# A third expert's products between the steps of a gated linear attention, with single buffers in exchange

## The chip, the cores and the metric

The kernel runs on one core of a Trainium2 chip. A core has five engines with a queue of instructions each: TensorE (PE: matrix products and, listed apart as PEld, the loads of their weights), VectorE (DVE), ScalarE (ACT), GpSimd (POOL) and SyncE (SP, which here issues nearly all DMAs). They wait for one another through semaphores. [...] The metric is the device time of one execution in microseconds (us).

## What is computed

A linear attention with a decaying state (4 batches, 8 heads, 768 tokens, head size 48), whose output is the input of eight dense experts (3072 tokens, width 384, inner width 1024), weighted by gates that a Sinkhorn iteration normalizes.

```python
for t in range(S):
    state = alpha[:, :, t, :, None] * state + einsum('bhd,bhe->bhde', k[:, :, t], v[:, :, t])
    y[:, :, t] = einsum('bhd,bhde->bhe', q[:, :, t], state)
...
logits = x @ w_gate                      # x: y with heads side by side
P = exp(logits - logits.max())
for _ in range(8):
    P /= P.sum(1, keepdims=True) + 1e-09
    P /= P.sum(0, keepdims=True) + 1e-09
    P *= N / E
for e in range(8):
    out += P[:, e:e+1] * (maximum(x @ w1[e], 0) @ w2[e])
```

## The kernel before

**Attention.** A unit is 256 tokens of a batch (12 units), a chunk 128 tokens (24 chunks, two a unit). For each unit `attn_block` (lines 238 to 377) loads q, k and alpha as `qt`, `kt`, `al` with a block of 16 tokens of one head on each partition, works out the scores inside the blocks over four levels (products on POOL or DVE as `tmp`, sums on DVE into `AB`, then `merge`), and puts the decayed q and k, the block decays (`ds`) and the scores through DRAM into another layout (`KN`, `QN`, `DN`, `an`); that put is its last step. It has 16 steps, each ended by a `yield`. `attn_decays` makes tables of decays from `DN` (the transpose psd on PE). `attn_chunk` (lines 419 to 534) has five steps for 128 tokens: transposes psk and psq and the decayed copies `decq`, `deck`; the products psl of whole blocks; the output psy, its largest value and the scaled copy `ys`; the transpose psx into `xT`, and the new state; the gate's logits psg (`lg`).

**Experts.** Values are split in two float16 halves, so each product is three. `moe_tile` (line 173) does one expert for a tile of tokens: eight groups of nine products `ps<-w,xT`, each taken out by ACT and DVE as the two halves `h`, and then, for each 128 tokens, 24 products of 384 columns `ps<-w,h`. Experts 0 and 1 are done while the attention runs, 256 tokens at a time, and their results go unweighted to DRAM (`raw`), since the gates aren't known yet. Their weights pass through the part of `xT` that late tokens will fill (lines 121 to 126). After the attention and the Sinkhorn iteration, experts 2 to 7 go in tiles of 512 tokens, one after the other; the first of them reads the two `raw` results of its tokens and weights them too (`evac_first`, line 679).

**Order.** While `hold` is set, every engine keeps program order. For the first chunks that order is written out by hand (START, line 39: `b1` a step of unit 1's block, `w0` one of expert 0's weights, `c0` one of chunk 0, `f` 0.45 us of the experts' products; a capital moves work from DVE to POOL). From chunk 3 on the loop of lines 608 to 626 takes five steps for each chunk, those of the chunk and the first two of the next in turn; after each step come two half steps, each with `fill(FILL / 2)`, which issues experts' products until their time by its count (0.96 us a piece) is used up, and `ahead`, which issues the steps of a later unit's block at fixed distances: its 16 steps begin 27 half steps ahead of its unit's first and end 12 ahead. `push` queues a unit's two tiles of 15.36 us, by the same count, at the third step of the unit's second chunk.

Of the kernel before, what the change touches and what calls it, by code (L numbers as in the profile page):

```python
# [8 lines left out]
F16 = mybir.dt.float16  # L9
# [10 lines left out]
EPS = 1e-9  # L20
# [3 lines left out]
def tile_gla_moe(ctx: ExitStack, tc: tile.TileContext, q, k, v, alpha, wg, w1, w2, out):  # L24
# [5 lines left out]
    U = 256                 # tokens of a unit of attention  # L30
    NU = S // U             # units of a batch
    NCH = U // P            # chunks of a unit
    KT_ = DM // P           # k tiles of the first product
    FT = FF // P            # f tiles
    NTT = NT // P           # token tiles
    NP = H // 2             # pairs of heads
    DP = 64                 # head dim, padded
    OFF = 28
    START = 'b1 W0 f W0 f f f w0 f f f f f f f c0 f f w0 W0 f B1 W0 b1 c0 f w0 f f W0 f c1 f f f f W1 f b1 c0 W0 c0 b1 f w0 w0 f f f w0 w0 f f c1 g b1 f f W1 c1 B1 W1 f f c0 f f b1 f f f f f f c1 f b1 f f B1 B1 f B1 W1 f f f f B1 B2 b1 w1 c1 f f f f f B1 w1 f b1 W1 W1 f f f w1 w1 w1 f b2 c2 w0 f w1 f f f B2 f f f f f B1 w1 W1 f f f w1 f f b2 f c2 B1 f f f f f f b2 f f w1 b2 f B2 f f f f B1 f b2 c3 f f f c2 b2 f f B2 f f B2 c3 f f f b2 f f c2 f B2 f B2 f f c2 f'.split()
    FILL = 3.0             # us of the experts' products between steps of the attention  # L40
# [5 lines left out]
    class Held:  # L46
        """an engine whose instructions stay in program order while hold is set"""
# [23 lines left out]
    cp = ctx.enter_context(tc.tile_pool(name="cp", bufs=1))  # L71
    sm = ctx.enter_context(tc.tile_pool(name="sm", bufs=4))
    wp = ctx.enter_context(tc.tile_pool(name="wp", bufs=2))

# [4 lines left out]
    mask = cp.tile([P, 8], F32, name="mask")          # mask[p, b] = (p // 16 == b)  # L79
# [10 lines left out]
    lg = cp.tile([P, NTT, E], F32, name="lg")          # logits, then P  # L90
    p2t = cp.tile([P, NTT], F32, name="p2t")           # power of two of each token
    wsc = cp.tile([P, E], F32, name="wsc")             # what undoes the scales of an expert

    def pow2_scale(mx, target, nm):
        """mx [P,1] >= 0 -> (float power of two <= mx, target / it)"""
# [15 lines left out]
    XT, W1T, W2T, WGT = 8.0, 4.0, 8.0, 8.0   # lower ends of the scaled maxima  # L111

    def load_expert(e, pool, res):
        """both weights of an expert, scaled and split into res; yields after its loads and each piece of work"""
        todo, pws = [], []
        for nm, w, target, C, W in (("w1", w1, W1T, KT_, FF), ("w2", w2, W2T, FT, DM)):
            src = w[e].rearrange("(c p) f -> p c f", p=P)
            hl = [wp.tile([P, C, W], F16, tag=f"{nm}{i}", name=f"{nm}{i}_{e}") for i in range(2)]
            n = -(-C // KT_)
            cut = [slice(i * n, min(C, (i + 1) * n)) for i in range(KT_)]  # L120
            if pool is None:
                # the first experts' weights pass through the room of late tokens
# [50 lines left out]
    def moe_tile(e, ws, t0, T, hp, evac):  # L173
        """yields the time of each piece of its products, in us"""
# [33 lines left out]
    raw = [dr.tile([NT, DM], F32, tag=f"raw{e}", bufs=1, name=f"raw{e}") for e in range(2)]  # L208
# [7 lines left out]
    hp1 = ctx.enter_context(tc.tile_pool(name="hp1", bufs=2))  # L216
# [6 lines left out]
    DN = [ap1.tile([16, H, DP], F32, name=f"DN{i}") for i in range(2)]  # L223
# [6 lines left out]

    for x in DN + ST:
        GE.memset(x, 0.0)
# [3 lines left out]
    ids = iter(range(1 << 20))  # L236

    def attn_block(b, u, got):
        """scores inside blocks of 16 tokens; a partition is a (block, head)"""
# [5 lines left out]
        qt = ap2.tile([P, 16, D], F32, tag="qt", name=f"qt_{nm}")  # L245
        kt = ap2.tile([P, 16, D], F32, tag="kt", name=f"kt_{nm}")
        al = ap2.tile([P, 16, D], F32, tag="al", name=f"al_{nm}")
# [6 lines left out]
        fast = g == 0                           # the first unit goes the shortest way  # L254
# [15 lines left out]
        def level(L):  # L270
            """what a level multiplies, and what then makes blocks of 2L"""
# [3 lines left out]
            # the decay over a block of L is kept at the block's first token  # L275
# [31 lines left out]
        if fast:  # L307
# [21 lines left out]
            for x in QN + KN:  # L329
                pool.memset(x[:, :, :, D:], 0.0)  # L330
        else:
            # what GpSimd multiplies is summed a step later
            t = mult(pool, "tmp4", [16], Af[:, 0:256:17], qt, kt)
            yield
            total(*t)
# [397 lines left out]
```

## Time and profile before

| | us |
|---|---|
| median of 3 runs | 1893.0 (1891.2 to 1894.6) |
| span of the profiled execution | 1885.1 |
| PE busy in it | 1722.3 |
| DVE busy | 893.8 |
| ACT busy | 464.4 |
| POOL busy | 346.3 |

The profile gives the profiled execution's span, from its first to its last instruction, and no total time of its own; the median of the runs lies 7.9 us above that span. Matmuls overlap in PE's pipeline, so a product's length in the trace is longer than its share of the time: how fast products follow one another is read from the starts in a timeline. Engines overlap too, so busy times don't add up to the span. [...]

### The profile page before, as it was taken

Reading aid. Unit: us, or ns where it says so; the run is one execution under the profiler, and the core shown is the slowest. Engines: PE = TensorE matmul, PEld = TensorE weight load, DVE = VectorE, ACT = ScalarE, POOL = GpSimd, SP = SyncE. Lnnn points to the kernel's source line nnn. Section 1 sums busy time; section 2 is a strip of 40 time slices with the busy share of each in tenths; the row PEclk is TensorE's granted clock in tenths of the full one; section 3 lists DMA queues with packets and bytes.
Section 4 is the critical chain, followed back from the end, with each engine's and each line's share of the span. In section 5 each row is a group of like instructions: output and inputs, shape, how many; then the busy total and the mean of one; then the engine's idle time right before and its main releaser. Section 6 shows DMA issues by size and latency. Waiting matters only on the chain.

```text
span 1885.1 us, 30215 instructions
## 1 busy us (share of the span) xinstructions
PE 1722.3 (91%) x13016; PEld 1064.5 (56%) x13016; DVE 893.8 (47%) x1723; ACT 464.4 (25%) x1008; POOL 346.3 (18%) x315
## 2 busy tenths in 40 slices
PE   0556889989889899999999999999999999999999
PEld 0435767767667786455555555555555555555555
DVE  6466766666676646952352235223423332323222
ACT  2232333333323242531221112111211121211111
POOL 4435545545455520000000000000000000000000
PEclk9867899999999999999999999999999999999999
DMA  6131233333333212640010001000100000000000
GB/s 177 57 82 46 50 89 91 87 88 92 91 76 79 68 37 85 210 134 0 34 34 1 1 34 34 1 1 34 34 1 1 1 1 1 1 1 17 34 17 34
DMA packets 143125, 92.20 MB, mean 49 GB/s; under 512 B 107152, under 2 KB 132240, under 8 KB 142992
## 3 DMA queue, kind: packets, MB, share of 16 engines
q1 hardware_dynamic: 142992, 90.28, 17.4%
q8 instruction: 102, 1.67, 0.4%
q14 instruction: 31, 0.25, 0.0%
HBM read 64.79 MB, written 25.46 MB: 48 GB/s over the span
## 4 chain that ended last, share of the span: by engine, by line
PE 65%; DVE 15%; DMA 7%; issue 5%; POOL 5%; ACT 2%; SPq 1%; POOLq 0%; ACTq 0%; DVEq 0%
PE ps L65 62%; POOL tmp L56 4%; DVE AB L56 3%; DMA kt<-in_k_dram 2%; DVE tmp L56 2%; DVE qt L56 2%; DMA ri<-raw 1%; DVE h L56 1%; PE psy L65 1%; DMA qs<-qt 1%; DVE decq L56 1%; DMA DN<-ds 1%; DVE w L56 1%; SPq L56 1%; DMA w2f<-in_moe_w_dram 1%
## 5 line engine op out<-in xcount | busy, mean ns | idle before, releaser
L65 PE MATMUL ps<-xT,w 128*128 128x512 f16 (+2 forms) x4392 | 785.1, 338 | 17.0 <-DVE h L56 11.1
L65 PE MATMUL ps<-w,h 128*128 128x384 f16 x4608 | 773.6, 328 | 10.6 <-DVE h L56 10.5
L65 PEld LDWEIGHTS <-w 128*128 128x128 f16 x4392 | 429.5, 100 | 351.0 <-issue 20.2
L65 PEld LDWEIGHTS <-h 128*128 128x128 f16 x4608 | 451.7, 98 | 308.5 <-issue 10.6
L56 ACT ACTIVATE h<-ps 128x512 f16<-128x512 f32 (+2 forms) x488 | 243.3, 505 | 898.8 <-PE ps L65 898.4
L56 DVE SCALAR_TENSOR_TENSOR h<-ps,h 128x512 f16<-128x512 f32 (+2 forms) x488 | 273.9, 574 | 362.8 <-ACT h L56 362.5
L56 DVE SCALAR_TENSOR_TENSOR acc<-ps,pe,acc 128x384 f32<-128x384 f32 x144 | 88.7, 616 | 360.7 <-PE ps L65 360.7
L56 POOL TENSOR_TENSOR tmp<-qt,kt 128x768 f32<-128x768 f32 (+1 forms) x88 | 152.2, 1734 | 152.7 <-DVE AB L56 61.7
L56 DVE TENSOR_REDUCE AB<-tmp 128x16 f32<-128x768 f32 (+2 forms) x105 | 94.6, 902 | 84.0 <-POOL tmp L56 83.5
L56 POOL PARTITION_ALL_REDUCE w1g<-w1m x8 | 2.9, 357 | 533.4 <-DVE w1m L56 521.8
L56 ACT COPY A<-psl 16x128 f32<-16x128 f32 (+2 forms) x168 | 56.0, 333 | 77.8 <-PE psl L65 66.4
L65 PE MATMUL psl<-decq,deck 48*32 48x32 f32 (+1 forms) x1152 | 33.7, 218 | 43.8 <-POOL deck L56 22.0
L65 PE MATMUL psy<-vn,A 128*128 128x48 f32 x384 | 58.1, 283 | 1.8 <-POOL w L56 1.8
L65 PEld LDWEIGHTS psy<-vn,A 128*128 128x128 f32 x384 | 54.9, 209 | 2.3 <-POOL w L56 2.2
L65 PEld LDWEIGHTS psl<-decq,deck 48*32 48x32 f32 (+1 forms) x1152 | 28.6, 129 | 46.3 <-POOL deck L56 22.6
L68 PE MATMUL psk<-ident,KN 128*128 128x128 f32 x96 | 17.4, 309 | 39.0 <-POOL KN L56 30.2
L56 POOL TENSOR_TENSOR kt<-kt,al 128x384 f32<-128x384 f32 x47 | 48.5, 1031 | 11.2 <-issue 7.1
L56 POOL TENSOR_TENSOR A<-an,mask 128x1024 f32<-128x1024 f32 x24 | 47.9, 1996 | 0.0
L56 DVE TENSOR_TENSOR qt<-qt,al 128x384 f32<-128x384 f32 (+1 forms) x55 | 46.4, 844 | 0.0
L56 ACT ACTIVATE ys<-psy,s_t 128x384 f32<-128x384 f32 x24 | 14.0, 581 | 131.4 <-DVE s_t L56 113.2
L65 PE MATMUL psy<-ST,Tq 128*128 128x96 f32 x160 | 35.2, 304 | 6.6 <-DVE wgm L56 6.2
L56 ACT COPY r<-ps 128x384 f32<-128x384 f32 x48 | 23.0, 479 | 69.3 <-PE ps L65 60.1
(139 smaller groups left out, 914.6 us busy)
## 6 DMA issues: line engine op xcount, KB each, us to landing
raw<-r SPq DMA_DIRECT2D x48, 192.0 KB, 1.9
w1f<-in_moe_w_dram SPq DMA_DIRECT2D x6, 1536.0 KB, 6.7
w2f<-in_moe_w_dram SPq DMA_DIRECT2D x6, 1536.0 KB, 6.9
ri<-raw SPq DMA_DIRECT2D x48, 192.0 KB, 2.5
qt<-in_q_dram SPq DMA_DIRECT2D x12, 384.0 KB, 4.3
al<-in_alpha_dram SPq DMA_DIRECT2D x12, 384.0 KB, 5.3
kt<-in_k_dram SPq DMA_DIRECT2D x12, 384.0 KB, 6.2
KN<-ks SPq DMA_DIRECT2D x24, 192.0 KB, 3.1
```

The costliest lines, as they stand in the source:

```text
L56: r = f(*a, **k_)
L65: tc.keep_in_program_order(nc.tensor.matmul(out_, lhsT, rhs, start=start, stop=stop))
L68: tc.keep_in_program_order(nc.tensor.transpose(out=out_, in_=in_, identity=idn))
```

## The change

NA = 3 experts are done beside the attention. The third one's weights come after START through the same part of `xT`, one step of `load_expert` after each step of a chunk from chunk 3 on, into a pool of their own (`wpa`). Its tiles wait in `late` until its weights are ready, and are queued with the others from then on, three tiles a unit. FILL goes from 3.0 to 4.7 us. To make room, `qt`, `kt`, `al`, `h`, `DN`, the decayed copies and `ys` have one buffer in place of two (the first unit's q, k and alpha are in a pool `first` that is closed early). A step of unit 2's block that START has ahead of unit 1's put now does that put. Sinkhorn has the load of expert 3 in front, and expert 3's preparation stands beside the last tiles. Five experts remain, and the first of them reads three `raw` results. The diff also drops comments; those lines are left out here.

```diff
-    FILL = 3.0             # us of the experts' products between steps of the attention
+    FILL = 4.7
+    NA = 3
...
+    early = ExitStack()
+    wpa = early.enter_context(tc.tile_pool(name="wpa", bufs=1, side="right"))
...
-            hl = [wp.tile([P, C, W], F16, tag=f"{nm}{i}", name=f"{nm}{i}_{e}") for i in range(2)]
+            hl = [(wpa if e == NA - 1 else wp).tile([P, C, W], F16, tag=f"{nm}{i}", name=f"{nm}{i}_{e}")
+                  for i in range(2)]
...
-    raw = [dr.tile([NT, DM], F32, tag=f"raw{e}", bufs=1, name=f"raw{e}") for e in range(2)]
+    raw = [dr.tile([NT, DM], F32, tag=f"raw{e}", bufs=1, name=f"raw{e}") for e in range(NA)]
...
-    hp1 = ctx.enter_context(tc.tile_pool(name="hp1", bufs=2))
...
-    DN = [ap1.tile([16, H, DP], F32, name=f"DN{i}") for i in range(2)]
+    DN = [ap1.tile([16, H, DP], F32, name="DN")] * 2
...
+    fst = ExitStack()
+    first = fst.enter_context(tc.tile_pool(name="first", bufs=1, side="right"))
...
-        qt = ap2.tile([P, 16, D], F32, tag="qt", name=f"qt_{nm}")
-        kt = ap2.tile([P, 16, D], F32, tag="kt", name=f"kt_{nm}")
-        al = ap2.tile([P, 16, D], F32, tag="al", name=f"al_{nm}")
+        qt, kt, al = ((first if g == 0 else ap1).tile([P, 16, D], F32, tag=x, name=f"{x}_{nm}")
+                      for x in ("qt", "kt", "al"))
...
-            t = ap2.tile([P, NP, m_ * L], F32, tag=f"dec{s}{L}", name=f"dec{s}{L}_{nm}")
+            t = ap2.tile([P, NP, m_ * L], F32, tag=f"dec{s}{L}", bufs=1, name=f"dec{s}{L}_{nm}")
...
-        ys = ap2.tile([P, DM], F32, tag="ys", name=f"ys_{nm}")
+        ys = ap2.tile([P, DM], F32, tag="ys", bufs=1, name=f"ys_{nm}")
...
-    wAB = [[], []]
-    w0, w1_ = (load_expert(e, None, wAB[e]) for e in range(2))
+    wAB = [[] for _ in range(NA)]
+    w0, w1_, w2_ = (load_expert(e, None, wAB[e]) for e in range(NA))
...
+    fst.close()
+    hp1 = early.enter_context(tc.tile_pool(name="hp1", bufs=1, side="right"))
...
-            advance(blocks[int(a[1])], 1)
-            done[int(a[1])] += 1
+            m = int(a[1])
+            if m == 2 and not got[1]:
+                m = 1
+            advance(blocks[m], 1)
+            done[m] += 1
...
+    late = [(2, 0, U)]
...
                 push((0, g * U, U), (1, g * U, U))
+                late.append((2, g * U, U))
             for z in range(2):
                 fill(FILL / 2)
                 ahead(10 * i + 2 * n + z)
+                if z and next(w2_, True):
+                    push(*late)
+                    late = []
...
-    w2_ = load_expert(2, wst, ws)
+    w3_ = load_expert(NA, wst, ws)
+    advance(w3_, 2)
     for n, _ in enumerate(sinkhorn()):
-        advance(w2_, n < 5)
         fill(2.8 if n else 4.0)
-    while len(filler) > 1:
+    while len(filler) > 3:
         fill(0.1)
     while filler:
-        advance(w2_, 1)
+        advance(w3_, 1)
         fill(1.0)
...
+    early.close()
+    hp2 = ctx.enter_context(tc.tile_pool(name="hp2", bufs=2, side="right"))
...
-        for i in range(2):
+        for i in range(NA):
...
-    for e in range(2, E):
+    for e in range(NA, E):
```

How instructions move is shown at three places. The first is POOL in the start, from the `p2t` or the last product of a level of unit 2's block to its later ones (`tmp_0_2_n` is the n-th product of that unit, `kt_2` its merge, `Tk_3` and `ST` belong to chunk 3). Before:

```order
L56 COPY p2t<-p_t_2_1284 128x1
L56 TENSOR_TENSOR kt_2_844<-kt_2_844,al_2_845 128x2x192
L56 TENSOR_TENSOR tmp_0_2_22_1322<-qt_2_843,kt_2_844 128x768
L56 TENSOR_TENSOR Tk_3_1235<-Tk_3_1235,k_0_1_988 128x512
L56 TENSOR_TENSOR ST_117<-ST_116,dtot_1_986 48x4x48 x2
L56 TENSOR_TENSOR tmp_0_2_23_1425<-qt_2_843,kt_2_844 128x768
```

And now:

```order
L57 TENSOR_TENSOR tmp_0_2_20_1304<-qt_2_975,kt_2_976 128x768
L57 TENSOR_TENSOR kt_2_976<-kt_2_976,al_2_977 128x2x192
L57 TENSOR_TENSOR tmp_0_2_21_1316<-qt_2_975,kt_2_976 128x1536
L57 TENSOR_TENSOR Tk_3_1238<-Tk_3_1238,k_0_1_992 128x512
L57 TENSOR_TENSOR tmp_0_2_22_1401<-qt_2_975,kt_2_976 128x768
L57 TENSOR_TENSOR ST_117<-ST_116,dtot_1_990 48x4x48 x2
L57 TENSOR_TENSOR tmp_0_2_23_1431<-qt_2_975,kt_2_976 128x768
```

The product of 1536 elements, `tmp_0_2_21`, stood on DVE before and is now POOL's, ahead of chunk 3's `Tk` and of the state `ST`.

The second is POOL in chunk 4, between two products of unit 3's block (`tmp_1_0_28` and `tmp_1_0_29`; `w1g` is a largest weight over all partitions, ISA alone a row without a name). Before:

```order
L56 TENSOR_TENSOR tmp_1_0_28_1782<-qt_0_1554,kt_0_1555 128x768
L56 COPY p2t<-p_t_4_1801 128x1
L56 TENSOR_TENSOR tmp_1_0_29_1824<-qt_0_1554,kt_0_1555 128x768
L56 TENSOR_TENSOR kt_0_1555<-kt_0_1555,al_0_1556 128x2x192
L56 TENSOR_TENSOR deck_0_5_1868<-Tk_5_1853,suf_124 128x256
```

And now:

```order
L57 TENSOR_TENSOR tmp_1_0_28_1835<-qt_0_1565,kt_0_1566 128x768
L57 ISA
L57 ISA w1g_1840<-w1m_2_1838 128x1
L57 COPY p2t<-p_t_4_1859 128x1
L57 ISA
L57 TENSOR_TENSOR tmp_1_0_29_1911<-qt_0_1565,kt_0_1566 128x768
L57 TENSOR_TENSOR kt_0_1566<-kt_0_1566,al_0_1567 128x2x192
```

The reduction of expert 2's first weights stands between them with a nameless row on either side; one for its second weights stands likewise ahead of chunk 6's `deck`.

The third is PE between the end of chunk 5's output (psy_5) and its transpose psx; `ps_e_t_m` are an expert's products for the tile from token t on, and psd, psk, psq belong to chunk 6. Before:

```order
L65 LDWEIGHTS h_1_256_1912
L65 MATMUL ps_1_256_1_2165<-w_1_622,h_1_256_1912 128x384
L68 MATMUL psd_0_2172<-ident,DN_115 128x16 x4
L68 MATMUL psk_0_2199<-ident,KN_113 128x128 x4
L68 MATMUL psq_0_2206<-ident,QN_111 128x128 x4
L65 LDWEIGHTS h_1_256_1911
```

And now:

```order
L66 MATMUL psy_5_2208<-ST_117,Tq_5_1965 128x96
L66 MATMUL psy_5_2208<-vn_2_1494,A_5_1975 128x48 x2
L69 MATMUL psd_0_2239<-ident,DN 128x16 x4
L69 MATMUL psk_0_2266<-ident,KN_114 128x128 x4
L69 MATMUL psq_0_2273<-ident,QN_112 128x128 x4
L69 MATMUL psx_5_2306<-ident,ys_5_2232 128x128 x3
```

Before, 18 products of expert 1 for the tokens from 256 on stand between psy_5 and psd, of which the last is shown, and more follow psq; now psd, psk, psq and psx follow psy_5 with none between. The same holds from the psl of chunk 5 on, but for 12 products right behind it.

## Rows read from the trace of the kernel before

**Rows 1.** The page's lines of the span and of PE, and the table of stretches: from and to (us), length, busy us of PE, PEld, DVE, ACT and POOL with their instructions, the granted clock of TensorE as a share of full speed, the mean busy share of the DMA engines, GB/s. The last row is one chunk near the end of the attention, from a call of its own.

```profile
span 1885.1 us, 30215 instructions
...
PE 1722.3 (91%) x13016; PEld 1064.5 (56%) x13016; DVE 893.8 (47%) x1723; ACT 464.4 (25%) x1008; POOL 346.3 (18%) x315
...
0.00:172.10 172.10, 78.42 (x936) 62.81 (x937) 109.07 (x187) 50.56 (x114) 84.30 (x88) 0.84 0.33 89
172.10:260.00 87.90, 71.32 (x818) 57.38 (x819) 50.47 (x99) 26.52 (x79) 35.75 (x32) 0.85 0.39 89
260.00:655.60 395.60, 353.43 (x4261) 278.37 (x4260) 271.79 (x507) 134.95 (x385) 211.87 (x172) 0.97 0.32 79
655.60:754.80 99.20, 96.74 (x958) 74.60 (x957) 53.94 (x159) 31.69 (x83) 10.54 (x14) 1.00 0.23 67
754.80:1881.30 1126.50, 1122.42 (x6050) 591.34 (x6047) 407.94 (x773) 220.73 (x348) 3.85 (x11) 1.00 0.08 27
...
667.46:689.31 21.85, 21.85 (x284) 18.06 (x283) 9.84 (x22) 8.77 (x22) 6.18 (x8) 1.00 0.06 20
```

**Rows 2.** The timeline of PE: start us, length us, engine, line, operation, out<-in, shapes, count, and in brackets the idle time just before and what ended it. The first products psy of chunks 3, 6 and 21.

```profile
172.11 0.71 PE L65 MATMUL psy<-ST,Tq 128*128 128x96 f32 x2 [0.36 <-DVE ST L56]
...
260.05 1.88 PE L65 MATMUL psy<-vn,A 128*128 128x48 f32 x16
...
655.59 0.36 PE L65 MATMUL psy<-ST,Tq 128*128 128x96 f32 x2
```

**Rows 3.** The experts' products (tile ps) on PE from 667.46 to 689.3 us, by their inputs: count, shortest, median and longest length in ns, first and last start in us.

```profile
L65 PE MATMUL ps<-xT,w x72: 270/272/273, 675.3 to 687.0; 128*128 128x256 f16 x72
L65 PE MATMUL ps<-w,h x42: 326/326/337, 667.5 to 688.0; 128*128 128x384 f16 x42
```

**Rows 4.** The timeline of PE, columns as in rows 2: two unbroken runs of an expert's products of 256 and of 384 columns, each with what follows it.

```profile
703.73 5.08 PE L65 MATMUL ps<-xT,w 128*128 128x256 f16 x45
708.64 1.14 PE L65 MATMUL ps<-w,h 128*128 128x384 f16 x6
...
709.94 6.01 PE L65 MATMUL ps<-w,h 128*128 128x384 f16 x36
715.79 0.37 PE L65 MATMUL psg<-wg,xT 128*128 128x8 f16 x9
```

**Rows 5.** The timeline of PE in the last six experts: the second products of one tile of 512 tokens, the first products of the next, and the start of its second.

```profile
772.50 15.76 PE L65 MATMUL ps<-w,h 128*128 128x384 f16 x96
788.10 15.70 PE L65 MATMUL ps<-xT,w 128*128 128x512 f16 x72
803.64 3.94 PE L65 MATMUL ps<-w,h 128*128 128x384 f16 x23
```

**Rows 6.** The waits of PE from 260 to 655 us: what waited, what for, us in total, times, longest us.

```profile
PE psl L65 <- DVE deck L56: 15.6, 7, 3.4
PE ps L65 <- DVE h L56: 10.6, 8, 5.1
PE psk L68 <- ACT ys L56: 8.1, 7, 1.8
PE psd L68 <- DMA DN<-ds: 5.7, 5, 1.5
PE pskn L68 <- DVE lg L56: 1.1, 3, 0.6
```

**Rows 7.** The timeline of PE: psd of units 2 and 3, and in the middle of the attention two waits, for ys and for deck.

```profile
187.34 0.58 PE L68 MATMUL psd<-ident,DN 16*128 16x16 f32 x4 [9.02 <-DMA DN<-ds]
...
242.19 0.42 PE L68 MATMUL psd<-ident,DN 16*128 16x16 f32 x4 [0.30 <-DMA DN<-ds]
...
422.27 0.65 PE L68 MATMUL psk<-ident,KN 128*128 128x128 f32 x4 [1.74 <-ACT ys L56]
...
433.98 1.93 PE L65 MATMUL psl<-decq,deck 48*32 48x32 f32 x48 [2.81 <-DVE deck L56]
```

**Rows 8.** The timeline of DVE in the same unit: an eviction of h, the first sum of a block behind its wait for POOL, and the product of 1536 elements.

```profile
406.60 0.42 DVE L56 SCALAR_TENSOR_TENSOR h<-ps,h 128x256 f16<-128x256 f32 x1 [2.28 <-ACT h L56]
411.32 0.95 DVE L56 TENSOR_REDUCE AB<-tmp 128x16 f32<-128x768 f32 x1 [4.30 <-POOL tmp L56]
...
428.20 3.45 DVE L56 TENSOR_TENSOR tmp<-qt,kt 128x1536 f32<-128x1536 f32 x1
```

**Rows 9.** The timeline of POOL: a reduction over partitions in the start and the product behind it, and in the middle of the attention the first product of a block.

```profile
67.33 0.38 POOL L56 PARTITION_ALL_REDUCE w2g<-w2m  x1 [6.00 <-issue]
74.60 0.98 POOL L56 TENSOR_TENSOR tmp<-qt,kt 128x384 f32<-128x384 f32 x1 [6.89 <-issue]
...
409.48 1.81 POOL L56 TENSOR_TENSOR tmp<-qt,kt 128x768 f32<-128x768 f32 x1 [6.93 <-DMA kt<-in_k_dram]
```

**Rows 10.** The timeline of the queue on SP: the issue of a unit's k load, of the first write of its put, and of the next unit's first load.

```profile
403.13 0.60 SPq L56 DMA_DIRECT2D kt<-in_k_dram  x1
...
441.52 0.57 SPq L56 DMA_DIRECT2D ks<-kt  x1
...
454.31 0.59 SPq L56 DMA_DIRECT2D qt<-in_q_dram  x1
```

**Rows 11.** The page's table of DMA issues: the loads of w1 outside the start, count, KB each, median us from issue to landing.

```profile
w1f<-in_moe_w_dram SPq DMA_DIRECT2D x6, 1536.0 KB, 6.7
```

More of the change, by code (lines that the diff above doesn't have):

```diff
@@ L229, in tile_gla_moe @@
                           for x, n in (("pre", 4), ("suf", 4), ("q32", 2), ("k32", 2)))
-    for x in DN + ST:
+    for x in DN[:1] + ST:
         GE.memset(x, 0.0)
@@ L626, in tile_gla_moe @@
                 ahead(10 * i + 2 * n + z)
+                if z and next(w2_, True):
+                    push(*late)
+                    late = []
     at.close()
     mp = ctx.enter_context(tc.tile_pool(name="mp", bufs=2))
-    hp2 = ctx.enter_context(tc.tile_pool(name="hp2", bufs=2))
     wst = ctx.enter_context(tc.tile_pool(name="wst", bufs=2))
@@ L663, in tile_gla_moe @@
     ws, wn = [], []
-    w2_ = load_expert(2, wst, ws)
+    w3_ = load_expert(NA, wst, ws)
+    advance(w3_, 2)
     for n, _ in enumerate(sinkhorn()):
-        advance(w2_, n < 5)
         fill(2.8 if n else 4.0)
-    while len(filler) > 1:
+    while len(filler) > 3:
         fill(0.1)
     while filler:
-        advance(w2_, 1)
+        advance(w3_, 1)
         fill(1.0)
-    advance(w2_, 99)
+    advance(w3_, 99)
     hold[0] = False
+    early.close()
+    hp2 = ctx.enter_context(tc.tile_pool(name="hp2", bufs=2, side="right"))
     T = 512
     def evac_first(e, tt, ps):
-        for i in range(2):
+        for i in range(NA):
             r = rp.tile([P, DM], F32, tag="raw", name=f"ri{i}_{tt}")
@@ L701, in tile_gla_moe @@
         for t0 in range(0, NT, T):
-            for _ in moe_tile(e, ws, t0, T, hp2, evac_first if e == 2 else evac_add):
+            for _ in moe_tile(e, ws, t0, T, hp2, evac_first if e == NA else evac_add):
                 next(more, None)
```

## The prediction

> **What bounds the kernel now.** I read four views in this order. First the page and the table of stretches [rows 1]: TensorE (PE) is busy 91% of the span. From 754.8 us on it is busy 1122.4 of 1126.5 us, so in the last six experts only less work would help. The idle time lies ahead of that, where the attention runs: 93.7 us are idle before 172.1 us, 16.6 in the next 87.9 us, 42.2 in the 395.6 us after that, 2.5 in the next 99.2. Second the chunk borders, the starts of the product psy [rows 2]: chunk 3 starts at 172.11, chunk 6 at 260.05, chunk 21 at 655.59 us, so chunks 6 to 20 take 395.5 / 15 = 26.4 us each. Third what a chunk costs PE when nothing waits: from 667.46 to 689.31 us, one chunk late in the attention, the engine is busy all of the 21.85 us [rows 1], and in these stand 42 experts' products of 384 columns and 72 of 256 [rows 3]. Their pace is (708.64 - 703.73) / 45 = 0.1091 us for 256 columns and (715.79 - 709.94) / 36 = 0.1625 us for 384, from the starts of two unbroken runs [rows 4], so the experts take 42 x 0.1625 + 72 x 0.1091 = 14.69 us of it and the attention 7.16 us. A tile of 256 tokens of one expert, 72 and 48 products, takes 7.86 + 7.80 = 15.66 us. The work of a chunk is then 7.16 + 15.66 (one tile for each of two experts per unit of two chunks) + 0.2 (half of a psd) = 23.0 us, and of 26.4 us some 3.35 are lost: 50.2 us in the 15 chunks. Fourth the waits of PE in that stretch [rows 6]: 41.1 us, of which 15.6 for deck, 10.6 for h, 8.1 for ys, 5.7 for DN, 1.1 for lg. The other 9 us are slower products, at a granted clock of 0.97 [rows 1].
>
> **The change part by part.** The same products are done before and after; a whole expert (12 tiles of 256 tokens) goes from the last stretch into the attention. So the sum is one of lost time, against the profiled span of 1885.1 us; the median of the runs shown, 1893.0 us, is 7.9 us above that span, and I add the same 7.9.
>
> *Shape.* At 512 columns a tile of 512 tokens took 803.64 - 772.50 = 31.14 us [rows 5], two tiles of 256 take 31.32: 6 x 0.18 = +1.1 us.
>
> *A, chunks 6 to 20.* FILL goes from 3.0 to 4.7 us in each of the five steps of a chunk. In the order on PE each wait has expert products ahead of it, now 1.7 us more per step. The wait for ys has one step's filler between psy and it and was 1.74 us at 422.27; the one for deck has two steps' (3.4 us more cover) and was 2.81 us at 433.98 [rows 7]. The cover removes both there, and DN's (5.7 us in five times, with four half steps of cover). What was late behind them was a chain of VectorE (DVE) and GpSimd (POOL): DVE stood 4.30 us for POOL's first product [rows 8], which stood 6.93 us for the k load [rows 9]; that latency stays, but each of the 15 half steps between a load and its put (403.13 to 441.52 us [rows 10], 2.6 us each) gets 0.5 us longer, so the lag is made up sooner. The waits for h aren't covered by filler: they are DVE's place in its queue, and the third expert adds eight evictions of 0.42 us [rows 8] a unit to DVE, which is busy 271.8 of 395.6 us [rows 1]. I leave 15 us lost (h's 10.6, a third of the 9, a little more): -35 us. Bounds: nothing gained, and all 50 gained; I take the value nearer to the second, since the last chunks of before, with no block beside them, leave PE busy for 21.85 of 21.85 us [rows 1].
>
> *B, the start.* The second unit's block may not be loaded before the first is put away, so its steps stand one later in the written order, and the product of 1536 elements falls on a step in capitals, which gives it to POOL. On DVE it takes 3.45 us [rows 8]; on POOL a product of half the size takes 1.81 us [rows 9], so 3.6 us. It stands ahead of the state update that psy of chunk 3 waits for: +3 us (0, where POOL waits anyway, to 7, twice it).
>
> *C, chunks 3 to 5.* Three things meet. The filler runs dry: unit 1's two tiles are 30.72 us by the count that fill keeps, enough for six steps at 4.7 and a part of the seventh. Behind the psl of chunk 5 stand 12 products, and from there until its psx none beside the attention (the third piece of order). Then the two reductions over partitions of expert 2 now fall among POOL's products of the attention. In the trace POOL stands 6.00 us ahead of such a reduction and 6.89 us behind it, with 0.38 us of its own: 13.3 us each [rows 9]; the order has a row ISA on either side. What ended both idle times is given as issue, nothing that the profile shows. [...] Last, the new expert's 1.5 MB of w1 are issued on SP ahead of unit 3's loads. The path: psd of unit 2 at 187.34, of unit 3 at 242.19 us, chunk 6 at 260.05 [rows 2, 7]. I add to the 54.9 us between the two psd 9 us for the first reduction (13.3 less some 4 in which POOL would have waited for DVE) and 3 for the loads (half of the 6.7 us in which a load of w1 lands [rows 11]). Behind the second psd the step's filler grows by 3 us and the second reduction costs 2, most of it under the wait for DN. Together 17 us, plus B. Of these 45.1 - 39.4 = 5.8 us are expert products done earlier (47 pieces of 0.96 us in chunks 3 to 5 by the rules of fill, and 41 before), work that the end is spared: C = +11 us. Bounds: +2, if the reductions hide in the dry stretch, and +28, if both 13.3 us stand on the path and the loads cost 6.
>
> *E, behind the attention.* Expert 3's weights are prepared beside 30.7 us of filler, where before it was 4.8 us beside expert 2's; the 2.5 us idle there may go. The first expert afterwards reads three partial results per tile of tokens and not two; the last stretch lost 1126.5 - 36 x 31.14 = 5.5 us, to be multiplied by up to 1.5. +1 us (-2 to +6).
>
> *One buffer each.* At nothing: a unit's put is issued from 441.52 and the next loads from 454.31 us on [rows 10], 12.8 us later, so the load doesn't meet its reader; h is free when PE, which works in order, has read it, before the next tile's first product is there; decq, deck and ys are read two steps before they are written again. If a load had to wait after all, its 6.93 us on POOL would move with it.
>
> Sum: 1885.1 + 1.1 - 35 + 3 + 11 + 1 = 1866.2; with 7.9 us **1874 us**.
>
> **The rivals.**
> *DVE's queue sets the pace (slower).* DVE keeps the order of the program here; an eviction of h stands behind a sum that waits for POOL. With three experts there are three passages a unit from the first product to the second, where PE needs all eight evictions. The trace shows one such wait of 5.1 us (the longest for h [rows 6]) and otherwise short ones; DVE is busy 69%. [...] If a chunk goes on losing 3.35 us, A is 0 and the time is 1874 + 35 = 1909 us. It decides from 16.1 / 15 = 1.1 us less gained, that is from 2.3 us lost a chunk on. Against it: the waits for deck, ys and DN are 29.4 of the 41.1 us.
> *The start eats it.* C at its upper bound: 1874 + 17 = 1891 us, no change. For it: 13.3 us twice on an engine that the attention waits for; against it: PE has no filler left to lose there and POOL is busy only 35.75 of 87.9 us [rows 1].
> *Half the cover.* The waits shrink by half, 25 us left: 1874 + 10 = 1884 us, still faster.
>
> **How the numbers follow.** My forecast 0.55, half the cover 0.15, the start 0.12, DVE's queue 0.18. Below 0.2%, 3.8 us, a change of this kernel can't be told from none: the first two are faster (0.70), the start is the same (0.12), DVE's queue is slower (0.18). The range starts between my value and all lower bounds (A 46, C 2, E -2 would be 1848), at 1856, and ends at 1903, where the slower case is half taken in; the forecast's own range is 1860 to 1888.
>
> **What would show it.** In the changed profile chunks 6 to 20 should take 31 to 32.5 us each (7.16 + 23.49 + 0.2 = 30.9 and what is lost), with the waits for deck, ys and DN nearly gone and the clock near 1. psy of chunk 6 should start near 280 us, with PE idle for some 8 us ahead of unit 3's psd. Two reductions between 200 and 275 us should have 6 to 7 us of POOL's idle time on each side. The stretch at full pace at the end should be five experts, some 934 us. Wrong would be: chunks over 33.1 us, or h as the first of PE's waits with more than 20 us.

## The result, and the profile after

The changed kernel took 1907.47 us (median of 4 runs, 1905.69 to 1911.88) beside 1892.38 us of the kernel before on the same chip: a ratio of 1.0078, with a 95% interval of 1.0061 to 1.0095. It is slower by 0.8%, where the forecast was 1874 us and faster, and it lies 4 us outside the range. In every run on record the time lies some 1.7 us above the span of the same execution (1908.3 and 1906.6 us for the profiled one here), so the kernel before, with its span of 1885.1 us, was profiled in an execution some 6 us faster than its median, and the spans differ by 21.5 us where the medians differ by 15.1.

The page and the table of stretches of the changed kernel, columns as in [rows 1]. The stretches have the same borders: psy of chunk 3, of chunk 6, of chunk 21, and the first 512-token tile.

```profile
span 1906.6 us, 31339 instructions
...
PE 1722.3 (90%) x13448; PEld 1107.4 (58%) x13448; DVE 892.9 (47%) x1770; ACT 482.6 (25%) x1080; POOL 349.4 (18%) x315
...
0.00:173.30 173.30, 78.66 (x937) 62.87 (x937) 103.83 (x186) 50.34 (x114) 84.18 (x87) 0.85 0.33 89
173.30:305.30 132.00, 81.29 (x854) 63.64 (x855) 67.30 (x128) 33.07 (x86) 40.52 (x36) 0.72 0.33 85
305.30:801.90 496.60, 473.88 (x5257) 373.39 (x5256) 296.64 (x571) 169.11 (x470) 210.95 (x170) 0.98 0.28 68
801.90:957.50 155.60, 150.23 (x1365) 114.43 (x1364) 83.74 (x221) 50.76 (x123) 11.63 (x17) 1.00 0.25 78
957.50:1904.00 946.50, 938.23 (x5042) 493.12 (x5039) 341.35 (x667) 179.28 (x288) 2.10 (x6) 1.00 0.10 30
```

PE's busy time is 1722.3 us in both kernels, so all of the 21.5 us between the two spans is idle time. It is in the second row: chunks 3 to 5 take 132.0 us and not 87.9, with PE busy for 62% of them and a granted clock of 0.72 in the mean. The third row has the third expert in it and loses 22.7 us in 496.6, where before 42.2 were lost in 395.6.

The waits of PE in chunks 6 to 20, columns as in [rows 6]:

```profile
PE ps L66 <- DVE h L57: 22.4, 9, 5.5
PE psq L69 <- DVE dT L57: 0.2, 1, 0.2
```

The waits for deck, ys, DN and lg [rows 6] are gone, as forecast; the one for h has doubled from 10.6 us. And the timeline of PE in chunks 3 to 5, columns as in [rows 2]: the waits that the kernel before has not, or not at this size (a wait of 9 us for DN ahead of the psd of unit 2 stands in both, [rows 7]).

```profile
197.85 0.37 PE L66 MATMUL ps<-xT,w 128*128 128x256 f16 x1 [4.14 <-ACT xT L57]
207.33 7.25 PE L66 MATMUL ps<-xT,w 128*128 128x256 f16 x44 [9.12 <-DVE xT L57]
...
256.64 2.08 PE L66 MATMUL ps<-w,h 128*128 128x384 f16 x6 [17.47 <-DVE h L57]
...
278.28 0.58 PE L69 MATMUL psd<-ident,DN 16*128 16x16 f32 x4 [5.97 <-DMA DN<-ds]
...
284.84 0.37 PE L66 MATMUL ps<-xT,w 128*128 128x256 f16 x1 [3.19 <-ACT xT L57]
286.96 6.71 PE L66 MATMUL ps<-xT,w 128*128 128x256 f16 x44 [1.75 <-DVE xT L57]
```

Each of the three chunks has a hole of its own: chunk 3 at 197 and 207 us, chunk 4 at 257, chunk 5 from 278 to 287. The experiments take them one by one. They ran on three chips, where the kernel before took 1892.0 us (no loads, no reductions, thin filler, nine buffers), 1890.5 and 1889.5; each ratio is to the kernel before on the same chip.

### The profile page after: what moved, and what is told of

Its sections match the earlier page's. It is cut to its first block, busy times and chain, and to the rows that moved or that the text cites. A ratio compares the mean times of both kernels' runs of the same rounds, so it can differ in the third digit from the quotient of the medians.

```text
span 1906.6 us, 31339 instructions
## 1 busy us (share of the span) xinstructions
PE 1722.3 (90%) x13448; PEld 1107.4 (58%) x13448; DVE 892.9 (47%) x1770; ACT 482.6 (25%) x1080; POOL 349.4 (18%) x315
## 4 chain that ended last, share of the span: by engine, by line
PE 73%; DVE 12%; DMA 5%; issue 4%; POOL 3%; ACT 2%; SPq 1%; POOLq 0%; ACTq 0%; DVEq 0%
PE ps L66 66%; PE psy L66 3%; DMA ri<-raw 2%; PE psl L66 2%; DVE AB L57 2%; POOL tmp L57 1%; DVE tmp L57 1%; DVE h L57 1%; DVE decq L57 1%; DVE w L57 1%; DVE w1m L57 1%; DVE acc L57 1%; DVE deck L57 1%; DMA w1f<-in_moe_w_dram 1%; DVE w2m L57 1%
## 5 line engine op out<-in xcount | busy, mean ns | idle before, releaser
L66 PE MATMUL ps<-w,h 128*128 128x384 f16 x4608 | 781.5, 329 | 48.1 <-DVE h L57 44.6
L66 PE MATMUL ps<-xT,w 128*128 128x256 f16 (+2 forms) x4824 | 781.3, 322 | 29.2 <-DVE xT L57 10.9
L66 PEld LDWEIGHTS <-w 128*128 128x128 f16 x4824 | 470.6, 99 | 320.2 <-issue 31.5
L57 DVE SCALAR_TENSOR_TENSOR h<-ps,h 128x256 f16<-128x256 f32 (+2 forms) x536 | 280.9, 536 | 402.4 <-ACT h L57 401.5
L57 ACT ACTIVATE h<-ps 128x256 f16<-128x256 f32 (+2 forms) x536 | 250.6, 475 | 813.9 <-PE ps L66 813.2
L57 DVE SCALAR_TENSOR_TENSOR acc<-ps,pe,acc 128x384 f32<-128x384 f32 x120 | 74.0, 617 | 301.4 <-PE ps L66 301.4
L57 POOL TENSOR_TENSOR tmp<-qt,kt 128x768 f32<-128x768 f32 (+2 forms) x89 | 153.4, 1728 | 183.4 <-DVE AB L57 77.7
L57 ACT COPY r<-ps 128x384 f32<-128x384 f32 x72 | 34.4, 477 | 157.9 <-PE ps L66 146.3
L66 PEld LDWEIGHTS psy<-vn,A 128*128 128x128 f32 x384 | 54.9, 209 | 2.4 <-POOL w L57 2.2
L57 POOL TENSOR_TENSOR kt<-kt,al 128x384 f32<-128x384 f32 x47 | 49.1, 1045 | 11.4 <-issue 7.1
L57 POOL TENSOR_TENSOR A<-an,mask 128x1024 f32<-128x1024 f32 x24 | 47.9, 1995 | 0.0
L57 DVE TENSOR_TENSOR qt<-qt,al 128x384 f32<-128x384 f32 (+1 forms) x55 | 42.2, 767 | 0.0
```

Source lines behind the costliest of these rows:

```text
L57: r = f(*a, **k_)
L66: tc.keep_in_program_order(nc.tensor.matmul(out_, lhsT, rhs, start=start, stop=stop))
```

## The experiments

**1. Is the third expert's density worth anything, or does DVE's queue set the pace of a dense chunk?**

```diff
-    FILL = 4.7
+    FILL = 3.0
```

> Changed kernel with the 3.0 us of filler per pair of steps that the kernel before has, in place of 4.7: the third expert still comes in, but half as dense and longer. Theory (idle time of chunks 6 to 20 is won by the density; chunks 3 to 5 hold their cost but for the dry part): chunks 6 to 20 go back to 26 to 28 us with some 50 us lost, 23 more than in the changed kernel, chunks 3 to 5 lose 8 to 16 less, the whole 1914 to 1924. Rival (VectorE's queue sets the pace of a dense chunk, so thinner is not worse): 1900 to 1910.

Measured: 1936.09 us, ratio to before 1.0225 [1.0205, 1.0246]; 29 us above the changed kernel and slower than both ranges. Its chunks 3 to 5 and 6 to 20, columns as in [rows 1], and its waits in chunks 6 to 20, as in [rows 6]:

```profile
173.20:299.00 125.80, 76.31 (x819) 59.95 (x820) 64.14 (x122) 32.20 (x85) 37.73 (x34) 0.74 0.34 87
299.00:694.50 395.50, 354.72 (x4259) 278.64 (x4258) 273.23 (x508) 134.28 (x385) 211.87 (x172) 0.96 0.33 79
```

```profile
PE psl L66 <- DVE deck L57: 15.4, 7, 3.4
PE ps L66 <- DVE h L57: 10.1, 5, 6.0
PE psk L69 <- ACT ys L57: 6.6, 8, 1.7
PE psd L69 <- DMA DN<-ds: 5.7, 5, 2.2
```

The reader should set these beside [rows 1] and [rows 6]: 395.5 us against 395.6, 4259 products against 4261, and the same waits to a few tenths (h) or to 1.5 us (ys). That the tiles of a third expert stand among the filler changes nothing there; what the changed kernel wins in these chunks comes from the density, with all the evictions that it adds to DVE. From chunk 6 to the end the thin version takes 1933.1 - 299.0 = 1634.1 us and the dense one 1906.6 - 305.3 = 1601.3; of these 32.8 us, 5.0 are products that the dense one had done before (PE busy 81.29 and 76.31 us in chunks 3 to 5). Some 28 us are won by density: 19 of them are idle time, the rest slower products (clock 0.96 and 0.98 in chunks 6 to 20). The rival on DVE's queue, by which a dense chunk would lose as much as a thin one, falls for these chunks. Chunks 3 to 5 lose only 6 us less than in the changed kernel, so what they cost is not the filler's amount in the main.

**2. Chunk 3: a transfer that the copies do not need.** In the changed kernel the two copies of chunk 3's tokens into xT wait for loads of the third expert's weights. The timelines of ACT, DVE and SP's queue, columns as in [rows 2]:

```profile
197.32 0.48 ACT L57 CAST xT<-psx 128x384 f16<-128x384 f32 x1 [5.68 <-DMA xT<-in_moe_w_dram]
...
206.72 0.56 DVE L57 TENSOR_TENSOR xT<-psx,xT 128x384 f16<-128x384 f32 x1 [11.64 <-DMA xT<-in_moe_w_dram]
...
190.74 2.55 SPq L57 DMA_DIRECT2D xT<-in_moe_w_dram  x3
...
195.29 1.70 SPq L57 DMA_DIRECT2D xT<-in_moe_w_dram  x3
```

By the code the first load (w1) goes to the room of tokens 1024 and later of xT[0], the second (w2) to that of tokens 768 and later of xT[1], and the copies write tokens 384 to 511. ACT's copy, into xT[0], starts 6.6 us behind the issue of the first load, and DVE's, into xT[1], 11.4 us behind the second. Two edits, the first without the loads, the second with all of them but later:

```diff
-                    SP.dma_start(a[i], src[:, c])
+                    if e < NA - 1:
+                        SP.dma_start(a[i], src[:, c])
```

> Changed kernel, but the loads of the third expert's weights into the staging are left out (the weights that its steps turn then are whatever lies in the tile, so those values differ). Theory (a wait on a transfer that nothing needs): in chunk 3 the copies into xT stand 11.6 us for a load of the third expert's weights, though the tokens they write lie outside the staging; without the loads psy of chunk 3 to psy of chunk 4 falls from 52.9 us to 40 to 42, and the whole from 1907 to 1893 to 1897. Rival (VectorE's queue sets the pace as soon as the third expert's evictions are in it): VectorE's next work is late anyway, the stretch stays above 49 us and the whole within 3 us of 1907.

```diff
-                if z and next(w2_, True):
+                if z and (i > 3 or n > 1) and next(w2_, True):
```

> Changed kernel, with the third expert's preparation begun at the third step of chunk 3 in place of its first, so that its loads are issued behind the copies into xT; nothing is left out. Theory (the wait on a transfer that the copies do not need was worth what leaving the loads out gave, 11 us): psy of chunk 3 to 4 at 41 to 43 us, the later chunks as in the changed kernel but the dry part of chunk 5 up to 4 us longer, the whole 1896 to 1901. Rival (the loads only move on to chunk 4's copies, or the preparation that ends later costs as much again): the whole above 1903.

Measured: without the loads 1896.62 us, 1.0028 [1.0013, 1.0042]; chunk 3 to 4 at 41.8 us in place of 52.9, every later chunk within 0.2 us of the changed kernel. With late loads 1898.64 us, 1.0042 [1.0027, 1.0057]; chunk 3 to 4 at 42.0, chunk 4 to 5 at 37.1 (6 less), but chunk 6 to 7 at 47.9, where the preparation now ends (9 more). The timeline of PE and DVE without the loads:

```profile
193.57 0.42 PE L66 MATMUL ps<-xT,w 128*128 128x256 f16 x1
195.67 4.64 PE L66 MATMUL ps<-xT,w 128*128 128x256 f16 x21 [1.68 <-DVE xT L57]
...
195.07 0.55 DVE L57 TENSOR_TENSOR xT<-psx,xT 128x384 f16<-128x384 f32 x1
```

DVE's copy starts 11.65 us earlier and waits for nothing. The theory holds in both: the wait costs 11 us. Why there is a wait no run shows. Both tiles are [128, 3, tokens], so a copy goes over all three planes, and between its first and its last address lie tokens that the loads write; that the wait comes from this is my guess.

**3. Chunk 4: the reductions on GpSimd.** Half of the 17.47 us for h comes from here (timelines of POOL, DVE and ACT of the changed kernel, columns as in [rows 2]):

```profile
235.46 0.38 POOL L57 PARTITION_ALL_REDUCE w1g<-w1m  x1 [5.84 <-DVE h L57]
...
243.15 1.79 POOL L57 TENSOR_TENSOR tmp<-qt,kt 128x768 f32<-128x768 f32 x1 [7.17 <-issue]
...
229.11 0.15 DVE L57 TENSOR_REDUCE w1m<-w1m 128x1 f32<-128x3 f32 x1
...
244.97 0.95 DVE L57 TENSOR_REDUCE AB<-tmp 128x16 f32<-128x768 f32 x1 [9.73 <-POOL tmp L57]
...
256.17 1.07 DVE L57 SCALAR_TENSOR_TENSOR h<-ps,h 128x256 f16<-128x256 f32 x3
...
249.05 1.15 ACT L57 ACTIVATE w<-xT,s_w 128x1024 f16<-128x1024 f32 x1 [14.27 <-DVE s_w L57]
```

POOL is idle for 5.84 us ahead of the reduction and 7.17 behind it, as in [rows 9]. The view puts the end of the first down to an eviction of h, which the reduction doesn't read; what it reads, w1m, was ready at 229.26 us, some 6 us earlier. What POOL does in the two idle times no run shows. DVE stands 9.73 us for the product behind it, then goes through everything that the program has ahead of h; ACT stands 14.27 us for the scale, with four evictions of h behind that wait. Three edits: no reductions; late loads and experiment 5's buffers with the reductions kept; and the same two with the maximum taken on TensorE, where the last two of a weight's three maxima also come in one step:

```diff
-            GE.partition_all_reduce(mg, m1, channels=P, reduce_op=bass.bass_isa.ReduceOp.max)
+            if e == NA - 1:
+                mg = m1
+            else:
+                GE.partition_all_reduce(mg, m1, channels=P, reduce_op=bass.bass_isa.ReduceOp.max)
```

> Changed kernel, but the two reductions over the partitions on GpSimd for the third expert are left out (each partition's own maximum is taken as the scale, so those values differ). [...] Rival (VectorE has too much to do in these chunks, the reduction only marks the place): the wait for h comes later in the same chunk, chunk 4 to 5 stays above 38 us, the whole above 1901.

> The changed kernel with late loads and the nine buffers, the third expert's reductions on GpSimd as in the changed kernel; nothing is left out. It parts the reductions from the other two causes of the best version so far (1887 us). Theory (the two effects add, and the reductions cost what is left): 1892 to 1896, chunk 4 to 5 near 37 us as with late loads alone, against 32.4 in the version with the product. Rival (once the loads come late, the reductions cost nothing any more): 1886 to 1889.

```diff
-                if i < KT_ - 1:
+                if i < KT_ - 1 and (e != NA - 1 or i == 0):
...
-            GE.partition_all_reduce(mg, m1, channels=P, reduce_op=bass.bass_isa.ReduceOp.max)
-            yield
+            if e == NA - 1:
+                dm = sm.tile([P, P], F32, tag="ws_d", bufs=1, name=f"{nm}d_{e}")
+                VE.tensor_scalar_mul(dm, ident, m1)
+                yield
+                pg = psm.tile([P, 512], F32, tag="psm", name=f"{nm}pg_{e}")
+                mm(pg[:, :P], ones, dm)
+                yield
+                VE.tensor_reduce(mg, pg[:, :P], axis=AX.X, op=ALU.max)
+            else:
+                GE.partition_all_reduce(mg, m1, channels=P, reduce_op=bass.bass_isa.ReduceOp.max)
+                yield
...
```

> The changed kernel with late loads, and also nine buffers for the first eviction's reads and, for the third expert, the maximum over partitions by a product with a diagonal matrix on TensorE in place of the reduction on GpSimd; nothing is left out. Theory (three separate causes, found one by one at 11, 8 and 5 us, the second only as far as the waits behind the reduction were GpSimd's): the sum, so 1882 to 1888, faster than the kernel before by 0.2 to 0.5 %. Rival (VectorE's and ScalarE's work for the third expert's weights is what holds chunk 4, and a step of TensorE in its place brings a wait of its own): no better than 1892.

Measured: without the reductions 1904.53 us, 1.0080 [1.0045, 1.0114], 8 us above the 1888 to 1896 that I had expected, and by that ratio no faster than the changed kernel (1.0078). Chunk 4 to 5 falls from 43.0 to 35.0 us, between my 29 to 33 and the rival's 38, chunk 5 to 6 gets 1.2 us longer, and a wait for h stays (timeline of PE):

```profile
245.92 2.08 PE L66 MATMUL ps<-w,h 128*128 128x384 f16 x6 [8.56 <-DVE h L57]
```

From psy of chunk 3 to the first 512-token tile its profile takes 7.3 us less than the changed kernel's, and the tiles behind it lose 3.5 again. Late loads and buffers with the reductions: 1895.13 us, 1.0028 [1.0015, 1.0042]. With the product in their place: **1887.41 us, 0.9979 [0.9968, 0.9990]**, faster than the kernel before by 0.2% and, by the ratios, some 19 us faster than the changed one. So the exchange of the two reductions for the product, the maxima drawn together with it, is worth 7 to 9 us (7.7 between the medians, 7.4 between the spans, 1893.0 and 1885.6 us, 0.49% by the ratios). Half of chunk 4's wait is POOL's. The other half is the place of h in DVE's order, as that rival said; how much of it is the third expert's was not tried by itself. In the best version PE still stands here, without any reduction (timelines of PE and DVE; w1d, w1pg and w1g are the product's diagonal matrix, its result and the maximum).

```profile
233.39 2.08 PE L66 MATMUL ps<-w,h 128*128 128x384 f16 x6 [6.50 <-DVE h L57]
235.27 0.63 PE L66 MATMUL w1pg<-w1d,ones 128*128 128x128 f32 x2
...
225.77 3.45 DVE L57 TENSOR_TENSOR tmp<-qt,kt 128x1536 f32<-128x1536 f32 x1
229.14 2.33 DVE L57 TENSOR_REDUCE w1m<-xT 128x1 f32<-128x1024 f32 x2
...
232.93 1.07 DVE L57 SCALAR_TENSOR_TENSOR h<-ps,h 128x256 f16<-128x256 f32 x3
...
239.49 0.29 DVE L57 TENSOR_REDUCE w1g<-w1pg 128x1 f32<-128x128 f32 x1
```

From 225.77 to 232.93 us DVE works without a pause, on the block's product (3.45 us), the third expert's maxima (2.33) and small steps, while h waits its turn.

**4. Chunk 5: filler used up.** In the changed kernel PE is busy for 25.2 of chunk 5's 36.1 us, at a granted clock of 0.76; before it was 21.8 of 23.9 us at 1.00. The edit is less filler per step in chunks 3 to 5, first in the changed kernel, then in the best version with 1.5 and 1.95:

```diff
-                fill(FILL / 2)
+                fill(FILL / 2 if i > 5 else 1.5)
```

> Changed kernel with 1.5 in place of 2.35 matmul groups per fill in chunks 3 to 5, so that the third expert's work lasts over them and is not used up in chunk 5. Theory (chunk 5 runs dry of filler, TensorE falls idle there and its clock with it): psy of chunk 5 to 6 falls from 36.1 us to 27 to 31, chunks 3 and 4 get cheaper by their missing pieces and pay them back later at 0.98 us each; the whole from 1907 to 1895 to 1901. Rival (the filler's amount does not matter, the waits for VectorE and the staging's loads do): the idle time of chunks 3 to 5 keeps its sum, the whole stays within 3 us of 1907.

> The version with late loads, nine buffers and the product in place of the reduction, and with 1.5 in place of 2.35 per fill in chunks 3 to 5; nothing is left out. Theory (its chunk 5, 36.8 us where the kernel before has 23.9 with as many pieces, is long because the filler is used up before the next unit's tiles are pushed): chunk 5 to 6 at 27 to 31, some 4 pieces moved behind, the stretch of chunks 3 to 5 falls from 109.7 us to 98 to 104; where the pieces behind fall on the chunks as they do now the whole is 1878 to 1884, where they fall badly (as with thin filler alone, where chunks 6 to 20 took 15.6 us more) it is 1890 to 1900. Rival (waits for VectorE's work on the third expert's weights hold chunk 5, filler or not): the stretch stays above 107.

> The same with 1.95 per fill in chunks 3 to 5. Theory: chunk 5 to 6 between the 36.8 us of 2.35 and what 1.5 gives, the stretch of chunks 3 to 5 at 102 to 108; chunks 6 to 20 differ by where the pieces fall, 497 to 512 us; the whole 1880 to 1897. Rival (the amount of filler does nothing in chunk 5): the stretch stays above 108.

Measured: 1923.66 us, 1.0167 [1.0124, 1.0210], a clear miss; 1896.39 us, 1.0035 [1.0022, 1.0048]; 1895.55 us, 1.0034 [1.0023, 1.0045]. Chunk 5 to 6 does fall: from 36.1 to 28.4 us, and in the best version from 36.8 to 28.5 and 31.3. But in the changed kernel chunk 4 to 5 grows from 43.0 to 49.1 us, so that chunks 3 to 5 together take 125.3 us and not 132.0, with 4.7 us of PE's work put off: 2.0 us won. The rows of chunks 3 to 5, of the best version and of the same with 1.5:

```profile
173.50:283.20 109.70, 80.54 (x859) 63.59 (x860) 63.10 (x128) 31.32 (x84) 39.89 (x35) 0.79 0.39 100
```

```profile
173.00:272.20 99.20, 75.57 (x822) 60.37 (x823) 60.25 (x119) 28.43 (x80) 37.22 (x32) 0.80 0.43 111
```

Of the 10.5 us between them 5.0 are PE's busy time, done later; 5.5 us is what the dry stretch cost there. It is given back in chunks 6 to 20. There each has 5255 products, and the best version loses 23.9 us to h, the thin one 31.9 (the stretch and the wait of the best version, then both of the thin one):

```profile
283.20:785.90 502.70, 475.51 (x5255) 373.51 (x5255) 301.69 (x575) 171.01 (x473) 209.57 (x169) 0.98 0.28 68
```

```profile
PE ps L66 <- DVE h L57: 23.9, 9, 7.2
```

```profile
272.20:788.30 516.10, 480.41 (x5256) 377.24 (x5255) 302.02 (x583) 172.29 (x474) 210.49 (x171) 0.97 0.27 68
```

```profile
PE ps L66 <- DVE h L57: 31.9, 13, 5.8
```

Same products, same filler per step, 13.4 us more: 8.0 of waits for h, 4.9 of slower products at a lower clock, the rest small waits. What differs, as I read it, is which piece of a tile falls beside which step of a block; no run tries that by itself. The changed kernel and its thin version show the same (22.4 us in 496.6, 30.6 us in 512.2).

**5. Behind the attention: three reads through three buffers.**

```diff
-            r = rp.tile([P, DM], F32, tag="raw", name=f"ri{i}_{tt}")
+            r = rp2.tile([P, DM], F32, tag="raw2", name=f"ri{i}_{tt}")
...
```

> Changed kernel with the inputs that the first eviction behind the attention reads back in nine buffers of their own in place of the three shared ones. Theory (the chain of load, use, load over three buffers sets the pace of the first 60 us of the 512-token tiles): those two tiles fall from 34 to 35 us each to 31 to 32 us, the stretch from the first 512-token tile to the end from 945.4 us to 938 to 941, and the whole from 1907 to 1900 to 1903. Rival (VectorE's own work in these evictions sets the pace): the stretch stays within 1.5 us of 945.4 and the whole with it.

Here rp2 is a pool of nine buffers. Measured: 1902.83 us, 1.0065 [1.0048, 1.0082], 4.6 us less than the changed kernel by the medians, with intervals of the two ratios that overlap; so the traces have to show it. The second and third 512-token tiles are these, in the changed kernel and then with nine buffers (timeline of PE):

```profile
989.24 9.88 PE L66 MATMUL ps<-xT,w 128*128 128x512 f16 x45
...
1012.40 12.04 PE L66 MATMUL ps<-w,h 128*128 128x384 f16 x73 [2.07 <-DVE pe L57]
1024.27 9.88 PE L66 MATMUL ps<-xT,w 128*128 128x512 f16 x45
...
1047.88 2.35 PE L66 MATMUL ps<-w,h 128*128 128x384 f16 x8 [1.39 <-DVE h L57]
```

```profile
991.40 7.93 PE L66 MATMUL ps<-xT,w 128*128 128x512 f16 x36
...
1009.31 15.76 PE L66 MATMUL ps<-w,h 128*128 128x384 f16 x96
1024.91 5.34 PE L66 MATMUL ps<-xT,w 128*128 128x512 f16 x24
1040.45 15.76 PE L66 MATMUL ps<-w,h 128*128 128x384 f16 x96
1056.05 6.21 PE L66 MATMUL ps<-xT,w 128*128 128x512 f16 x28
```

The tiles take 35.0 and 37.2 us (the third ends at 1061.43) with three buffers, and 33.5 and 31.14 with nine: 7.5 us won, of which the stretch ahead of the first of these tiles gives 3 or 4 back, for a reason that no run shows.

**6. The single buffers and the redirected steps alone, in the kernel before.**

```diff
-    hp1 = ctx.enter_context(tc.tile_pool(name="hp1", bufs=2))
+    hp1 = ctx.enter_context(tc.tile_pool(name="hp1", bufs=1))
...
-    DN = [ap1.tile([16, H, DP], F32, name=f"DN{i}") for i in range(2)]
+    DN = [ap1.tile([16, H, DP], F32, name="DN")] * 2
...
+        qt, kt, al = ((first if g == 0 else ap1).tile([P, 16, D], F32, tag=x, name=f"{x}_{nm}")
+                      for x in ("qt", "kt", "al"))
...
```

> The kernel before, with the single buffers alone: h, q, k, alpha, DN, the decayed tiles and ys have one buffer each, the first unit its own q, k and alpha, and steps of unit 2 before unit 1 is ready go to unit 1; no third expert beside the attention, 3.0 us of filler as before. Theory (one buffer each costs nothing, the redirected steps 0 to 3 us): 1891 to 1896. Rival (the single buffers are part of what the changed kernel lost, in chunks 3 to 5 above all): above 1900.

Measured: 1892.65 us, 1.0003 [0.9990, 1.0016]; chunks 3 to 5 take 88.3 us, and the single buffers cost nothing that can be measured. From psy of chunk 2 to psy of chunk 3 it is 22.1 us, as in the changed kernel, and 18.6 before: that delay comes with the buffers and the redirected steps, without any third expert. But the steps ahead of chunk 2 are 2 us shorter in both, so psy of chunk 3 starts at 173.73 us here, at 173.28 in the changed kernel and at 172.11 before.

## Why the prediction was wrong

By its own terms, against the profiled span of 1885.1 us:

| term | forecast | measured | from |
|---|---|---|---|
| shape | +1.1 | +1.1 | not measured by itself |
| A, chunks 6 to 20 | -35 | -28 | lost 54.9 and 26.8 us: by the prediction's pace 1044 products of 256 columns and 716 of 384, then 1656 and 1100, and 7.36 us a chunk for the attention |
| B, start | +3 | +1.2 | psy of chunk 3 at 173.3 |
| C, chunks 3 to 5 | +11 | +38.2 | 132.0 - 87.9, less 6 pieces of 0.98 us done earlier |
| E, behind the attention | +1 | +9 | the rest of the 21.5 us |
| single buffers | 0 | 0 | experiment 6 |

The measured terms hang on one profile of the kernel before. Against experiment 6's (span 1891.4 us), which has the single buffers and the redirected steps but no third expert, A is -31, B 0, C +38 and E +8. The 7.9 us that the prediction carried over from the kernel before are not an overhead: the changed kernel's median lies 0.9 us above its span. So the forecast is off by 33 us: C 27, A 7, E 8, less 2 for B and 7 for this. The sum for the range's lower end takes A at 46 where the term's bound was 50; nothing here hangs on it.

**A was right in its mechanism and 4 to 7 us off.** The waits that filler covers went, and experiment 1 shows that density did it, with some 28 us. I also wrote that h as the first of PE's waits with more than 20 us would prove me wrong; it is, with 22.4. What was mis-sized is that wait: it grew with the density by 12 us, which the term had at "a little more", yet the waits that went were larger. The chunks took 33.1 us and not 31 to 32.5, the edge that I had set.

**B held where it was placed**: 3.5 us from chunk 2 to 3, as forecast, and 2 won ahead of it that it did not see.

**C is the step that failed**, by 27 us and by 10 beyond its upper bound. By the runs:

- 11.1 us in chunk 3 (132.0 less 120.9 without the loads). The prediction looked at the loads as 3 us of SP's queue ahead of unit 3's. It did not ask who writes the tile into which they are staged while they are under way.
- 7 us for the reductions (132.0 less 124.9; 7 to 9 for the exchange in experiment 3). Here the size was near, and on the high side: 9 and 2 had been booked. But the place was another. The prediction put the delay, some 8 us, ahead of unit 3's psd; there PE stood 5.97 us, and the larger wait stood in front of h, through DVE's and ACT's program order: 17.47 us, of which 8.56 stay without the reductions.
- 2 us for the dry stretch in chunk 5, 5.5 in the best version, seen in the order of the program but not priced by itself.

These are 20 to 24 of the 38 us; 14 to 18 stay open. The third expert's work on DVE and ACT, its maxima, scales and splits between evictions of h, **was booked at nothing**, and the 8.56 us for h are a place where it takes part, but no run leaves it out. Nor does the best version with thin filler price it. Its chunks 3 to 5 take 11.3 us more than before (99.2 and 87.9 us, with 822 and 818 products): 4.3 are slower products at a granted clock of 0.80 against 0.85, and 7.0 more are idle time. PE's waits there for the third expert's product and for h are these (columns as in [rows 6]), where the kernel before has none and 1.3 us:

```profile
PE w1pg L66 <- DVE w1d L57: 6.3, 1, 6.3
...
PE ps L66 <- DVE h L57: 0.4, 1, 0.4
```

PE stands there for the diagonal matrix of the product that took the reduction's place, since that product stands in PE's own order and DVE makes its matrix behind the block's product and the maxima. DVE is busy 61% of that stretch, so I take the place in the order to be the cause and not the load in the mean.

The rival on DVE's queue thus named a mechanism that took part, but in the wrong place: in chunks 6 to 20, where I priced it, what it keeps is the 22.4 us for h, less than was won, and it holds a part of chunk 4. That its 1909 us is near the result is chance.

**E missed its upper bound.** The stretch at full pace did begin with five experts, but 945 us (PE ends near 1903) and not 934: its loss was forecast as 5.5 us times 1.5 at most and was 11, since three loads for each 128 tokens pass through three buffers in turn. Experiment 5 shows it for the second and third tile. Another 2.9 us are lost in the row ahead of it (5.4 us idle against 2.5). That this is DVE's work on expert 3's weights beside the last tiles is argued only.

On the two idle times around a reduction, forecast as 6 to 7 us each, the trace agrees: 5.84 and 7.17 us around the first, 6.34 and 7.41 around the second (timeline of POOL of the changed kernel). There are two idle times each time, and the second of the first reduction, 7.17 us, is the one behind which DVE stood 9.73 us.

```profile
279.88 0.38 POOL L57 PARTITION_ALL_REDUCE w2g<-w2m  x1 [6.34 <-DVE e L57]
287.67 0.61 POOL L57 TENSOR_TENSOR deck<-Tk,suf 128x256 f32<-128x256 f32 x1 [7.41 <-issue]
```

## What to carry to other kernels

When preparation work is moved in beside latency-bound work, price its place in each engine's program order and not its busy time: ask for each of its waits which eviction stands behind it. When a tile's idle room is lent out as staging, list who writes any part of that tile while the loads are under way, and issue the loads behind them. A gain from more filler is real and can be read from the waits it covers, but the stretch in which the new filler gets ready has to be charged to it: here it cost more than all that was won, and mending three places in it and behind it turned 0.8% slower into 0.2% faster.

## What was not expected of the hardware and the program

Equal work took 502.7 and 516.1 us in chunks 6 to 20, with 5255 products each and a granted clock of 0.98 and 0.97; I read the 13 us as the place of the filler's pieces against the steps of the attention. Thinner filler in three chunks changed all fifteen behind them. And a reduction over 128 partitions whose own row shows 0.38 us left POOL idle for 5.84 us ahead of it and 7.17 us behind it. Two of these reductions exchanged for a product with a diagonal matrix on TensorE (two matmul instructions, 0.63 us) and a maximum of 0.29 us on DVE gave 7 to 9 us of the whole kernel back, though PE then waits for DVE's matrix.
